# Sliding-window attention and feed-forward on one core: scores of six blocks in two steps, the mask table later, the order laid anew

## The chip, the cores and the metric

The kernel runs on one core of a Trainium2 chip. The metric is device time in microseconds (us), the median of several executions. Five engines work side by side, each through its own list of instructions, in order: TensorE (PE) multiplies matrices into PSUM, ScalarE (ACT) evaluates functions, VectorE (DVE) and GpSimd (POOL) work elementwise, SyncE (SP) issues transfers. ACT and POOL can issue transfers too.

## What is computed

Attention of 8 heads over 8 sequences of 576 rows, each row seeing itself and the 127 rows before it, with a bias that falls linearly with distance; then a normalised two-layer feed-forward part with a residual.

```python
# q, k, v: (8, 8, 576, 64) float32; scale = 1 / sqrt(64); window = 128
scores = scale * np.matmul(q, k.transpose(0, 1, 3, 2))
rel = pos[:, None] - pos[None, :]
slopes = 2.0 ** (-8.0 * (np.arange(H) + 1) / H)
bias = slopes[:, None, None] * (-np.abs(rel))[None]
mask = (rel >= 0) & (rel < window)
scores = np.where(mask, scores + bias, -1e9)
attn = softmax(scores)                      # (written out in the reference)
x = np.matmul(attn, v)                      # heads side by side: (8, 576, 512)
xn = (x - mean) / np.sqrt(var + 1e-06) * g_ln
out = x + np.maximum(xn @ w_ch1, 0.0) @ w_ch2     # w_ch1: 512 x 2048, w_ch2: 2048 x 512
```

## The kernel before

The 4608 rows are 36 blocks of 128 rows. Attention goes block by block; the feed-forward part goes by chunks of two to four blocks (`CHUNKS`). Every piece of work is a task with its dependencies, a rank `v` and assumed costs; a small planner in the kernel places the tasks on the engines, and the instructions are emitted in the order that it finds. So constants such as costs, ranks and `PICK` (which engine may do a task of which block) alter the order of the whole program. While PE would have nothing to do in the first 26 us of the plan, the kernel puts in filler matmuls on `warm_t`.

For one block (cut):

```python
CHUNKS = [2, 3, 4, 3, 4, 4, 4, 4, 4, 4]
BY_BIAS = 6       # blocks 0 to 5: the bias and mask come by a matmul (Z)
QK_BY_DMA = 13    # from this block on q and k are transposed by DMA, not by PE
X_BY_DMA = 11     # the same for x
SPANS = [0, 2, 5, 7]   # pairs of blocks whose q and k come in one transfer

scs = [psum.tile([P, 2, 512], FP32, ...) for n in range(2)]   # two score tiles
fb = {n: psum.tile([P, 512], FP32, ...) for n in range(4)}    # four banks for all else
plan.banks["sc"] = [0]      # both score tiles are handed out as one

# q, k, v loaded (SP), cast to 16 bit (POOL or ACT), q and k transposed on PE
# into a bank of fb, copied into qkt (DVE or ACT); then:

def e_s(e, b):                       # scores of both halves (four heads each)
    for half in range(2):
        for slot in range(2):
            for side in (() if r == 0 else (0,)) + (1,):   # block before, own block
                for g in range(2):
                    nc.tensor.matmul(scs[half][:, g, c0 : c0 + P], kt[rows, 1, hp, :],
                                     qkt[i][rows, 0, hp, :], start=not bias, stop=True, ...)
def e_z(e, b):                       # bias: scaled identity times distance table
    for half in range(2):
        for slot in range(2):
            for g in range(2):
                nc.tensor.matmul(scs[half][:, g, ...], sid[:, h, :], dist_t[:, kind, lo:],
                                 start=slot == 0, stop=False, ...)
if bias:
    z_ = [add(f"Z{i}", ("PE", ...), e_z, ..., acq=("sc", f"S{i}"))]
s_ = add(f"S{i}", ("PE", ...), e_s, z_ + qkt_done[i] + prev, ..., acq=("sc", f"S{i}"))
for half in range(2):
    # exp of one half: score tile -> probs (ACT)
    ex = add(..., e_x, [s_], ..., rel=f"S{i}")     # both give the score tiles back
    # from block 6 on: probs *= mask table (DVE or POOL)
# value products of each half (pv, PE), division (DVE), statistics, xs = (x - mean) * g (DVE),
# xs transposed (PE, then ACT or DVE; or by DMA) into xt
```

The mask table is made by ACT (eight instructions, `mreg`) and copied and cleared in two variants by POOL:

```python
for bank in range(4):
    for slot in range(2):
        # emit: nc.scalar.activation(mreg[:, bank, slot, :], dist_t[:, 0, :], AF.Exp, scale=-slope)
        tm.append(add(f"mreg{bank}{slot}", ("ACT", 0.4), emit, [d_dist[0]], av(MASK_AT, -10.0)))
# mmix and mnew: four copies and three memsets on POOL, which depend on tm
```

The weights come in eight transfers that POOL issues, which also convert to 16 bit; each stands behind a named cast:

```python
W_AFTER = [8, 14, 14, 14, 17, 18, 18, 20]   # 3 * block + (0: q, 1: k, 2: v)
# n < 4: a quarter of w1; n >= 4: a quarter of w2
```

The feed-forward part of a chunk (cut):

```python
for f in range(16):
    # A: 4 matmuls w1sb[:, kb, f] x xt[c] into a bank of fb; then relu -> ht (ACT or DVE)
for j in range(nb):
    # B: 16 matmuls ht x w2sb into a bank, in groups of four; then
    # ot = bank * rstd + xb (DVE), and the store (SP)
```

Of the kernel before, what the change touches and what calls it, by code (L numbers as in the profile page):

```python
# [16 lines left out]
class Task:  # L17
    __slots__ = ("eng", "emit", "deps", "v", "lat", "acq", "rel", "left", "users", "ready", "end", "start", "name", "room")

    def __init__(self, name, eng, emit, deps, v, lat, acq, rel):  # L20
        self.name, self.eng, self.emit, self.v, self.lat = name, eng, emit, v, lat
        self.deps = [d for d in deps if d is not None]
        self.acq, self.rel = acq, rel
        self.users, self.ready, self.end, self.start, self.room = [], 0.0, None, None, 0.0
# [22 lines left out]
class Plan:  # L47
# [36 lines left out]

    SLACK = (0, 0.4, 0)

# [13 lines left out]
    def run(self):  # L100
# [36 lines left out]
        def bank(t):  # L137
            if t.acq is None or t.acq[1] in held:
                return True, None
            open_ = [(when, b) for b, when in state[t.acq[0]].items() if when is not None and when <= now + 1e-9]  # L140
            return (True, min(open_)[1]) if open_ else (False, None)

        while left:
# [10 lines left out]
            for e in engines:  # L154
# [24 lines left out]
                if t.room:  # L179
                    used["DMA " + e] += t.room  # L180
                if t.acq is not None and t.acq[1] not in held:
                    held[t.acq[1]] = (t.acq[0], b)
                    state[t.acq[0]][b] = None
                if t.rel is not None:
                    waits[t.rel] -= 1
                    if waits[t.rel] == 0:
# [3 lines left out]
                        n += 1  # L190
                self.order.append((t, e, held[t.acq[1]][1] if t.acq is not None else None))
                left -= 1
# [26 lines left out]
def kernel(  # L219
# [10 lines left out]
    nc = tc.nc  # L230
# [12 lines left out]
    CH = CB * P  # L243
    CHUNKS = [2, 3, 4, 3, 4, 4, 4, 4, 4, 4]
    FIRST = [sum(CHUNKS[:c]) for c in range(len(CHUNKS))]
# [24 lines left out]
    SPAN = 36.0  # L270
    LEAD = 1.45
    WARM = 26.0
    SPANS = [0, 2, 5, 7]
    SLACK = (0.1, 0.4, 0.5)
    PICK = {('xt', 0): 'ACT DVE', ('xt', 8): 'ACT', ('cv', 5): 'POOL ACT', ('cv', 0): 'POOL', ('ev', 8): 'DVE', ('ev', 1): 'DVE', ('mkb', 8): 'DVE', ('mkb', 3): 'POOL', ('mka', 2): 'DVE', ('mkb', 4): 'POOL', ('ev', 3): 'ACT', ('mka', 0): 'DVE', ('ck', 8): 'ACT', ('mkb', 0): 'POOL', ('cq', 5): 'POOL', ('ev', 5): 'DVE', ('ck', 2): 'POOL', ('ck', 7): 'ACT', ('mkb', 6): 'POOL', ('mka', 5): 'DVE', ('cq', 6): 'POOL ACT', ('cq', 2): 'POOL ACT', ('xt', 6): 'ACT DVE', ('mka', 7): 'DVE', ('cq', 8): 'ACT', ('xt', 5): 'DVE', ('mka', 6): 'POOL', ('cv', 7): 'POOL ACT', ('cv', 3): 'POOL', ('xt', 3): 'ACT DVE', ('mka', 4): 'POOL', ('mka', 3): 'POOL', ('ev00', 4): 'DVE', ('cs1', 1): 'POOL', ('cs0', 0): 'POOL ACT', ('ev10', 3): 'DVE', ('xt', 2): 'ACT', ('cq', 3): 'POOL', ('cs0', 8): 'POOL ACT', ('ev01', 8): 'DVE', ('ev10', 8): 'ACT', ('ev11', 5): 'ACT', ('cs0', 2): 'POOL ACT', ('cq', 4): 'POOL', ('ev00', 8): 'DVE', ('ev01', 0): 'ACT', ('cv', 8): 'ACT', ('ev11', 0): 'ACT', ('cv', 4): 'POOL', ('mkb', 5): 'POOL', ('ev01', 6): 'DVE', ('cv', 6): 'ACT', ('ev10', 5): 'DVE ACT', ('cs1', 4): 'POOL ACT'}
    BY_BIAS = 6
    MASK_AT = 6
    QK_BY_DMA = 13
    X_BY_DMA = 11

# [45 lines left out]
    fb = {n: psum.tile([P, 512], FP32, tag=f"fb{n}", name=f"fb{n}") for n in range(4)}  # L326
    plan.banks["sc"] = [0]
    plan.banks["fb"] = list(fb)
# [18 lines left out]
    def load(name, src, r, i, v, slot=None):  # L347
        slot = i if slot is None else slot
        got = []
        for p0, n, b, s0 in where(i):  # L350
            def emit(e, bank, p0=p0, n=n, b=b, s0=s0):
                nc.sync.dma_start(  # L352
                    out=r[slot][p0 : p0 + n, :, :],
                    in_=src[b, :, s0 : s0 + n, :].rearrange("h p d -> p h d"),
                )
            t, d = plan.transfer(f"{name}{i}", "SP", 0.6, 1.22 * n / P, n / P, emit, (), v)
            r.writes(slot, t)
            got.append(d)
        return got
# [6 lines left out]
    for t in vx.tiles:  # L366
# [4 lines left out]
        plan.transfer(  # L371
            f"dist{n}", "ACT", 0.5, 0.15 * (k1 - k0), 0.0,
            lambda e, b, k0=k0, k1=k1: nc.scalar.dma_start(out=dist_t[:, k0:k1, :], in_=dist_dram.ap()[:, k0:k1, :]), deps, v,
# [25 lines left out]
    for bank in range(4):  # L399
        for slot in range(2):  # L400
            def emit(e, b, bank=bank, slot=slot):
                nc.scalar.activation(
                    out=mreg[:, bank, slot, :], in_=dist_t[:, 0, :], func=AF.Exp,
                    scale=-float(slopes[head_of(bank, slot)]),
                )
            tm.append(add(f"mreg{bank}{slot}", ("ACT", 0.4), emit, [d_dist[0]], av(MASK_AT, -10.0)))
    tmix, tnew = [], []
# [46 lines left out]

    W_AFTER = [8, 14, 14, 14, 17, 18, 18, 20]
    t_w = {}
# [14 lines left out]

    span_done = {}
    qkt_done, vx_done, aggr_done, xs_done, xt_done = {}, {}, {}, {}, {}

    def attention(i):
# [33 lines left out]
        if i in span_of:  # L509
            n = span_of[i]  # L510
            if SPANS[n] == i:
                evs = [[], []]
                for a, r_, w_ in ((0, qs, qs16), (1, ks, ks16)):
                    key = f"T{i}.{a}"

                    def e_c(e, b, r_=r_, w_=w_):
                        dst = w_[n][:, :, :, :]
                        src = r_[n][:, :, :].rearrange("p h (t d) -> p t h d", t=2)
                        if e == "POOL":
                            nc.gpsimd.tensor_copy(out=dst, in_=src)  # L520
                        else:
                            nc.scalar.activation(out=dst, in_=src, func=AF.Copy)
                    cs = add(f"c{key}", pick(f"cs{a}", "POOL", POOL=1.25, ACT=1.02), e_c, [span_load[n][a]], av(i, 0.1 * a))
                    r_.reads(n, cs); w_.writes(n, cs)

# [54 lines left out]

        def e_s(e, b):
            for half in range(2):
                for slot in range(2):
                    hp = 2 * half + slot
                    for side in (() if r == 0 else (0,)) + (1,):
                        for g in range(2):
                            rows = slice(D * g, D * g + D)
                            kt = qkt[i - 1 + side]
                            c0 = slot * 2 * P + side * P
                            nc.tensor.matmul(  # L590
                                scs[half][:, g, c0 : c0 + P],
                                kt[rows, 1, hp, :],
                                qkt[i][rows, 0, hp, :],
                                start=not bias,
                                stop=True,
                                skip_group_check=True,
                            )

        pr = []
        def e_z(e, b):  # L600
            for half in range(2):
                for slot in range(2):
                    for g in range(2):
                        h = head_of(2 * half + g, slot)
                        nc.tensor.matmul(
                            scs[half][:, g, slot * 2 * P + lo : slot * 2 * P + 2 * P],
                            sid[:, h, :],
                            dist_t[:, kind, lo:],
                            start=slot == 0,
                            stop=False,  # L610
                            skip_group_check=True,
                        )
        if bias:
            z_ = [add(f"Z{i}", ("PE", 0.87 if r else 0.46), e_z, t_sid + [d_dist[kind > 0]], av(i, 1.5), acq=("sc", f"S{i}"))]
        else:
            z_ = []
        s_ = add(f"S{i}", ("PE", 0.64 if r else 0.42), e_s, z_ + qkt_done[i] + prev, av(i, 2.0), acq=("sc", f"S{i}"))
        qkt.reads(i, s_)
        if r:
            qkt.reads(i - 1, s_)  # L620
        for half in range(2):

            def e_x(e, b, half=half):
# [5 lines left out]
                nc.scalar.activation(out=o, in_=n_, func=AF.Exp, scale=inv_sqrt_d)  # L629
            ex = add(f"ex{'ab'[half]}{i}", ("ACT", 1.02 if r else 0.62), e_x, [s_], av(i, 2.4 + half), rel=f"S{i}")  # L630
            probs.writes(i, ex)
# [12 lines left out]
        for half in range(2):  # L644
            key = f"V{'ab'[half]}{i}"

            def e_pv(e, b, half=half):
                pp = fb[b]
                for hh in range(4):
                    h = 4 * half + hh  # L650
                    bank, slot = 2 * half + h % 2, (h % 4) // 2
                    for side in (() if r == 0 else (0,)) + (1,):
# [8 lines left out]
                     [pr[half], cv] + ([vx_done[i - 1]] if r else []), av(i, 5.0 + half), acq=("fb", key))  # L661
            probs.reads(i, pv)
            vx.reads(i, pv)
            if r:
# [69 lines left out]
        if j == CHUNKS[c] - 1:  # L734
# [10 lines left out]
            lv.writes(c, ln); lv.reads(c, rs); mv.reads(c, ln); rstd.writes(c, rs)  # L745
            for n in range(nb):
                mv.reads(c, xs_done[FIRST[c] + n])
            kept[c] = rs
# [59 lines left out]
    for i in range(NBLK):  # L808
        attention(i)
    for c in range(len(CHUNKS)):  # L810
        mlp(c)
# [46 lines left out]
```

The softmax here doesn't subtract the row's maximum and nothing guards it: scores larger than these inputs give would overflow.

## Time and profile before

| | |
|---|---|
| time, median of 3 | 327.29 us (326.95 to 329.19) |
| span of the profiled execution | 326.8 us |
| PE busy | 317.4 us |
| ACT, DVE, POOL busy | 162.2, 186.0, 81.1 us |
| A (line 762), 640 matmuls | 135.2 us |
| B (line 788), 576 matmuls | 133.2 us |
| mean granted PE clock | 0.993 |
| HBM read, written | 36.93 MB, 9.44 MB |

The page gives busy times of the engines over the whole span and in 40 equal slices. The durations of matmuls overlap, so rates are read from runs of them in the timeline. A bracket behind a timeline row is the idle time before it and what ended it. Times of transfers run from issue to landing. Bias matmuls are line 605, scores 590, value products 653; transposes of q and k 530 (spans) and 555, of x 713; the filler is 817.

### The profile page before, as it was taken

The page shows a single profiled execution, that of the slowest core. Times are in us where ns is not written, and L with a number is a line of the kernel's source. Part 1 is how long each engine was busy: PE and PEld are TensorE (multiplying, and loading weights), DVE is VectorE, ACT ScalarE, POOL GpSimd, SP SyncE. Part 2 cuts the span into 40 slices and gives each one's busy share as a digit, 9 for nine tenths or more (in the row PEclk, how much of TensorE's full clock was granted, in tenths as well). Part 3 has the DMA queues.
Part 4 walks back from the last instruction along what each step waited for, and adds up shares of the span by engine and source line. Part 5 has one row for each costly group of instructions (what it writes and reads, how often), then busy time and mean ns, then how long its engine had stood idle before and what let it go on. Part 6 is the DMA issues. An engine that isn't in the chain of part 4 may idle for free.

```text
span 326.8 us, 6755 instructions
## 1 busy us (share of the span) xinstructions
PE 317.4 (97%) x2678; PEld 174.4 (53%) x2678; DVE 186.0 (57%) x402; ACT 162.2 (50%) x259; POOL 81.1 (25%) x116
## 2 busy tenths in 40 slices
PE   8996999999999999999999999999999999999995
PEld 7985865555554565454454544444444444444442
DVE  2284871797664299485685686566556745520011
ACT  5864964633760385376237632772276237405600
POOL 1775192443120431231600505210000000000000
PEclk9997999999999999999999999999999999999999
DMA  8999999997999999999999999934222320121011
GB/s 206 232 191 256 215 216 215 225 197 210 226 204 237 189 221 197 238 234 187 185 252 182 186 215 231 171 55 127 91 40 50 96 82 1 21 79 64 0 66 64
DMA packets 151955, 51.93 MB, mean 159 GB/s; under 512 B 134770, under 2 KB 147314, under 8 KB 151923
## 3 DMA queue, kind: packets, MB, share of 16 engines
q1 hardware_dynamic: 147264, 47.07, 69.1%
q0 software_dynamic: 4224, 4.19, 7.9%
q8 instruction: 21, 0.34, 0.5%
q10 hardware_dynamic: 434, 0.23, 0.3%
q14 instruction: 12, 0.09, 0.1%
HBM read 36.93 MB, written 9.44 MB: 142 GB/s over the span
## 4 chain that ended last, share of the span: by engine, by line
PE 84%; DMA 5%; SPq 4%; issue 2%; POOL 2%; DVE 0%; ACT 0%; POOLq 0%
PE fb L788 38%; PE fb L762 36%; PE sc L590 5%; PE fb L653 4%; DMA v<-in_v_dram 4%; SPq L352 3%; DMA k<-in_k_dram 1%; POOL probs L636 1%; SPq L428 1%; PE fb L555 1%; POOL w2sb L468 0%; PE fb L713 0%; PE fb L530 0%; ACT qkt L544 0%; DVE ot L796 0%
## 5 line engine op out<-in xcount | busy, mean ns | idle before, releaser
L762 PE MATMUL fb<-xt,w1sb 128*128 128x512 f16 (+2 forms) x640 | 135.2, 359 | 0.1
L788 PE MATMUL fb<-w2sb,ht 128*128 128x512 f16 x576 | 133.2, 379 | 0.0
L774 ACT ACTIVATE ht<-fb 128x512 f16<-128x512 f32 (+2 forms) x138 | 77.3, 562 | 92.6 <-PE fb L762 90.9
L762 PEld LDWEIGHTS <-w1sb 128*128 128x128 f16 x640 | 59.4, 98 | 56.1 <-issue 0.7
L629 ACT ACTIVATE probs<-sc 128x1024 f16<-128x1024 f32 (+1 forms) x72 | 67.8, 973 | 35.2 <-PE sc L590 32.6
L788 PEld LDWEIGHTS <-ht 128*128 128x128 f16 x576 | 53.4, 98 | 59.4
L796 DVE SCALAR_TENSOR_TENSOR ot<-fb,rstd,xb 128x512 f32<-128x512 f32 x36 | 26.9, 748 | 54.8 <-PE fb L788 54.4
L504 POOL CAST vx<-v 128x512 f16<-128x512 f32 x33 | 20.9, 638 | 112.9 <-PE fb L653 83.3
L636 DVE TENSOR_TENSOR probs<-probs,mreg 128x1024 f16<-128x1024 f16 (+1 forms) x46 | 31.3, 684 | 19.7 <-ACT probs L629 19.7
L673 DVE TENSOR_TENSOR xb<-fb,rec 128x256 f16<-128x256 f32 x72 | 30.0, 422 | 2.0
L653 PEld LDWEIGHTS <-probs 128*128 128x128 f16 x544 | 24.5, 98 | 11.8 <-POOL probs L636 0.7
L701 DVE SCALAR_TENSOR_TENSOR xs<-xb,mv,g_t 128x512 f16<-128x512 f16 x36 | 29.8, 829 | 1.1
L669 DVE RECIPROCAL rec<-fb 128x4 f32<-128x4 f32 x72 | 12.3, 176 | 28.7 <-PE fb L653 28.5
L653 PE MATMUL fb<-vx,probs 128*128 128x65 f16 x544 | 27.0, 194 | 0.4 <-POOL probs L636 0.4
L490 POOL CAST qk<-q 128x512 f16<-128x512 f32 x28 | 19.8, 709 | 29.1 <-DMA qkt<-qk 12.4
L690 DVE BATCH_NORM_STATS2 st<-xb 128x6 f32<-128x512 f16 x36 | 24.9, 691 | 0.9
L490 POOL CAST qk<-k 128x512 f16<-128x512 f32 x28 | 19.5, 695 | 9.0 <-DMA k<-in_k_dram 9.0
L590 PEld LDWEIGHTS <-qkt 64*128 64x128 f16 x544 | 15.6, 95 | 10.7 <-issue 9.6
L590 PE MATMUL sc<-qkt 64*128 64x128 f16 x288 | 19.7, 219 | 0.1
L590 PE MATMUL sc<-qkt,qkt 64*128 64x128 f16 x256 | 18.4, 221 | 0.0
L772 DVE TENSOR_SCALAR ht<-fb 128x512 f16<-128x512 f32 (+2 forms) x22 | 12.7, 579 | 6.5 <-PE fb L762 5.3
L817 PE MATMUL fb<-warm_t 128*128 128x128 f16 x176 | 13.3, 239 | 1.0 <-DVE warm_t L363 1.0
(47 smaller groups left out, 120.2 us busy)
## 6 DMA issues: line engine op xcount, KB each, us to landing
out_dram<-ot SPq DMA_DIRECT2D x36, 256.0 KB, 2.5
v<-in_v_dram SPq DMA_DIRECT2D x32, 256.0 KB, 4.9
q<-in_q_dram SPq DMA_DIRECT2D x24, 256.0 KB, 4.8
k<-in_k_dram SPq DMA_DIRECT2D x24, 256.0 KB, 4.6
qs<-in_q_dram SPq DMA_DIRECT2D x4, 512.0 KB, 7.6
ks<-in_k_dram SPq DMA_DIRECT2D x4, 512.0 KB, 8.2
w1sb<-in_moe_w_ch_dram POOLq DMA_DIRECT2D x4, 512.0 KB, 9.0
w2sb<-in_moe_w_ch_dram POOLq DMA_DIRECT2D x4, 512.0 KB, 9.7
```

The source lines that it names most:

```text
L490: en.tensor_copy(out=qk16[nrm[i]][:, a, :], in_=s)
L590: nc.tensor.matmul(scs[half][:, g, c0 : c0 + P], kt[rows, 1, hp, :], qkt[i][rows, 0, hp, :], start=not bias, stop=True, skip_group_check=True,
L629: nc.scalar.activation(out=o, in_=n_, func=AF.Exp, scale=inv_sqrt_d)
L636: en.tensor_tensor(out=pv, in0=pv, in1=mask[:, 2 * half : 2 * half + 2, :, lo:], op=ALU.mult)
L653: nc.tensor.matmul(pp[:, hh * (D + 1) : hh * (D + 1) + D + 1], probs[i][:, bank, slot, side * P : side * P + P], vx[i - 1 + side][:, h, 0 ...
L673: nc.vector.tensor_tensor(out=xb[i][:, 256 * half : 256 * half + 256].rearrange("p (h d) -> p h d", d=D), in0=pp[:, :, 0:D], in1=rec[2 * i ...
L690: nc.vector.bn_stats(out=st[i][:, :], in_=xb[i][:, :])
L701: nc.vector.scalar_tensor_tensor(out=xs[i][:, :], in0=xb[i][:, :], scalar=mv[c][:, j, 0:1], in1=g_t[:, :], op0=ALU.subtract, op1=ALU.mult,)
L762: nc.tensor.matmul(fb[b][:, 0:n_], w1sb[:, kb, f * P : f * P + P], xt[c][:, kb, 0:n_], start=(kb == 0), stop=(kb == NKB - 1),)
L774: nc.scalar.activation(out=ht[c][:, f, 0:n_], in_=src, func=AF.Relu)
L788: nc.tensor.matmul(pm[:, :], ht[c][:, f, j * P : j * P + P], w2sb[:, f, :], start=(f == 0), stop=(f == NFB - 1),)
L796: nc.vector.scalar_tensor_tensor(out=ot[i][:, :], in0=fb[plan.held[key][1]][:, :], scalar=rstd[c][:, j : j + 1], in1=xb[i][:, :], op0=ALU. ...
```

## The change

Four things are altered together.

- Each of the two score tiles is handed out by itself, and for blocks 0 to 5 the bias and scores of the two halves are separate tasks: the first half's exponential may start when its own scores are there, and the next block's bias may enter the first tile when that tile is read.
- The mask table's ACT instructions depend on block 1's value products, so that they no longer stand at the start of the program.
- The order is laid anew: other assumed costs of transfers and casts, other choices of engine, other places of the weights' transfers, chunks of other sizes at the start, rank offset `LEAD` 1.5 for 1.45.
- q and k are transposed by DMA from block 12 on instead of 13, x from block 13 on instead of 11.

The diff, cut (helpers of the planner that let a task take two tiles, and most of `PICK`, left out):

```diff
-    CHUNKS = [2, 3, 4, 3, 4, 4, 4, 4, 4, 4]
+    CHUNKS = [2, 3, 3, 4, 4, 4, 4, 4, 4, 4]
-    LEAD = 1.45
+    LEAD = 1.5
+    TABLE_AFTER = 1
+    SPLIT = 6
-    PICK = {... ('ck', 7): 'ACT', ('mkb', 6): 'POOL', ('ev00', 8): 'DVE' ...}
+    PICK = {... ('ck', 7): 'POOL ACT', ('mkb', 6): 'DVE', ('ev00', 8): 'DVE ACT', ...
+            ('ev', 0): 'ACT', ('cv', 2): 'POOL ACT', ('ev00', 2): 'ACT', ('ev00', 7): 'ACT', ('ev10', 2): 'DVE'}
-    QK_BY_DMA = 13
-    X_BY_DMA = 11
+    QK_BY_DMA = 12
+    X_BY_DMA = 13
-    plan.banks["sc"] = [0]
+    plan.banks["sc0"] = [0]
+    plan.banks["sc1"] = [0]
-            t, d = plan.transfer(f"{name}{i}", "SP", 0.6, 1.22 * n / P, n / P, emit, (), v)
+            t, d = plan.transfer(f"{name}{i}", "SP", 0.6, 1.24 if n == P else 0.76, n / P, emit, (), v)
-            tm.append(add(f"mreg{bank}{slot}", ("ACT", 0.4), emit, [d_dist[0]], av(MASK_AT, -10.0)))
+            tm.append(add(f"mreg{bank}{slot}", ("ACT", 0.4), emit, [d_dist[0]], av(MASK_AT, 0.0)))
-    W_AFTER = [8, 14, 14, 14, 17, 18, 18, 20]
+    W_AFTER = [11, 13, 14, 14, 17, 18, 18, 22]
...
-        if bias:
-            z_ = [add(f"Z{i}", ..., acq=("sc", f"S{i}"))]
-        s_ = add(f"S{i}", ..., z_ + qkt_done[i] + prev, av(i, 2.0), acq=("sc", f"S{i}"))
+        pr, s_ = [], {}
+        for halves in ((0,), (1,)) if i < SPLIT else ((0, 1),):
+            acq = [(f"sc{hf}", f"S{i}{hf}") for hf in halves]
+            if bias:
+                z_ = [add(f"Z{tag}{i}", ..., e_z(halves), ..., av(i, 1.5 + 0.6 * halves[0]), acq=acq)]
+            st_ = add(f"S{tag}{i}", ..., e_s(halves), z_ + qkt_done[i] + prev, av(i, 2.0 + 0.6 * halves[0]), acq=acq)
+            for half in halves:
+                s_[half] = st_
-            ex = add(..., e_x, [s_], av(i, 2.4 + half), rel=f"S{i}")
+            ex = add(..., e_x, [s_[half]], av(i, 2.4 + half), rel=f"S{i}{half}")
...
     for i in range(NBLK):
         attention(i)
+        if i == TABLE_AFTER:
+            for t in tm:
+                t.deps.append(pv_done[i])
```

## The prediction

> **What bounds the kernel now.** I read the page's first two parts, then the engines' busy time by stretches of 2.5 us, then the timelines of TensorE, ScalarE and GpSimd over the first 50 us, then landing times of single transfers (the DMA view cut to narrow windows).
>
> ```profile
> PE 317.4 (97%) x2678; PEld 174.4 (53%) x2678; DVE 186.0 (57%) x402; ACT 162.2 (50%) x259; POOL 81.1 (25%) x116
> ...
> PE   8996999999999999999999999999999999999995
> ```
>
> TensorE (PE) is at 9 in nearly every slice. Only the fourth slice (24.5 to 32.7 us) drops to 6, and the last to 5. So nothing in the middle can be won by removing waits; either work leaves PE, or the stretch ahead of the full load gets shorter. By stretches (us, then PE, PEld, DVE, ACT, POOL busy, granted clock, DMA share, GB/s):
>
> ```profile
> 22.50:25.00 2.50, 2.50 (x49) 2.13 (x46) 2.08 (x7) 1.41 (x2) 1.21 (x2) 1.00 1.14 285
> 25.00:27.50 2.50, 0.00 (x0) 0.00 (x0) 0.63 (x1) 0.53 (x1) 0.86 (x1) 1.00 1.23 278
> 27.50:30.00 2.50, 2.27 (x28) 1.93 (x29) 1.22 (x3) 0.84 (x2) 2.50 (x4) 0.77 1.25 207
> 30.00:32.50 2.50, 2.50 (x31) 1.98 (x30) 1.30 (x3) 1.45 (x3) 0.57 (x2) 0.55 1.22 267
> ```
>
> PE is idle for a whole stretch, and in the two after it gets 0.77 and 0.55 of its clock. Before 25 us it is only nominally full: much is filler on `warm_t`. PE's timeline (start, length, engine, line, operation, count, wait before):
>
> ```profile
> 23.71 1.29 PE L817 MATMUL fb<-warm_t 128*128 128x128 f16 x20
> 27.73 0.62 PE L530 MATMUL fb<-iden,qs 128*128 128x128 f16 x8 [2.73 <-POOL qs L520]
> ...
> 31.71 0.61 PE L762 MATMUL fb<-xt,w1sb 128*128 128x256 f16 x2
> ```
>
> The first product of the feed-forward part (A, line 762) starts at 31.71. The transposes at 27.73 belong to blocks 5 and 6, which A of the first chunk does not need, but PE takes its instructions in order, and everything behind them waits. GpSimd's timeline shows what they waited for:
>
> ```profile
> 18.09 0.88 POOL L466 DMA_DIRECT2D w1sb<-in_moe_w_ch_dram  x1
> ...
> 22.96 0.75 POOL L466 DMA_DIRECT2D w1sb<-in_moe_w_ch_dram  x1
> 26.64 1.04 POOL L520 CAST qs<-qs 128x1024 f16<-128x1024 f32 x1 [2.93 <-DMA qs<-in_q_dram]
> 27.62 1.48 POOL L466 DMA_DIRECT2D w1sb<-in_moe_w_ch_dram  x2
> ```
>
> The q span of blocks 5 and 6 had not landed. And ScalarE at the start:
>
> ```profile
> 5.23 1.95 ACT L402 ACTIVATE mreg<-dist_t 128x256 f16<-128x256 f16 x6 [3.21 <-DMA dist_t<-dist]
> 7.09 1.04 ACT L522 ACTIVATE qs<-qs 128x1024 f16<-128x1024 f32 x1
> ```
>
> The first q span was issued at 0.75 and took 4.2 us to land (4.95), but its cast waited behind six mask table instructions until 7.09.
>
> **What the Trainium skill says.** "DMA: Bandwidth & Descriptors", section "Issuing engines are not separate DMA queues": transfers started by different engines share the same 16 DMA engines and interleave. The trace agrees: the first q span landed in 4.2 us, the fourth, issued at 26.53 amid four weight transfers from GpSimd's queue, in 16.8. "TensorE: Matmul & The Clock Gate", section "What's actually happening": the array's clock halves after an idle window of about 3.4 us. Here 2.73 us without a matmul were enough for grants of 0.77 and 0.55. Same page, section "Back-to-back issue gap": a warm matmul of N columns costs N / 2.4 + 2.5 ns, 215.8 ns for 512. The trace's last 64 take 13.83 us, 0.216 each; I use such rates, not the 379 ns of the page's groups, which overlap.
>
> **The change, part by part.**
>
> *1. PE's work from the first A to the end.* I counted matmuls in the two built programs' orders and priced them from the timeline: A 0.108, 0.162, 0.216 us for 256, 384, 512 columns; B 0.216; score 0.0347 (16 in 0.55); value product 0.0325 (8 in 0.26); bias 0.109 (8 in 0.87); transposes 0.0565 (8 in 0.45) and 0.055 (4 in 0.22). Before: 286.9 us behind the first A. After: 286.6. Block 12's q and k transposes leave PE (8 x 0.0565 = 0.45 saved), those of x of blocks 11 and 12 come to it (8 x 0.055 = 0.44); four bias and eight value matmuls move ahead of A and eight span transposes behind it. Worth 0.3. Before really took 322.7 - 31.7 = 291.0, so gaps cost 4.1, which I keep except below.
>
> *2. When A starts.* The new order does not put the transposes of blocks 5 and 6 ahead of A; they stand behind its first 16 matmuls. So the 2.73 us wait no longer blocks. Filler falls from 176 to 138 matmuls, at 0.056 us 2.1 us that the author no longer expects to wait. By hand along ScalarE, with durations from its timeline (exponential 0.97, evacuation 0.67, table entry 0.33):
> - Block 0 doesn't move (score at 11.45): the cast of q goes to GpSimd, free at 4.95, but 48 + 21 filler matmuls stand ahead of its transposes, where 47 + 15 stood.
> - Block 1: its bias into the first tile needs only the first exponential; score at about 13.7 for 14.46, exponentials from 14.1 for 15.18.
> - Block 2: behind two evacuations, x's evacuation and two table entries, exponentials from 18.7 for 19.61. Here the table, now behind block 1's value products, gives back 0.66.
> - Block 3: from 21.5 for 23.59, with three table entries (1.0) between its halves, and two more behind the second.
> - Block 4: first half from 25.1, for 31.40, its value product at 26.3, four bias matmuls, then A at about **26.7** for 31.71. The first weights were issued at 18.09 behind the same cast in both orders and took 7.2 us: 25.3, just in time.
>
> Gain 5.0. With the idle gone the clock should not sag; before, A's first 16 matmuls took 2.17 for 1.73: another 0.4.
>
> *3. What then ends the wait: the arrivals.* Adding up PE work in each order from its first A gives how far in each arrival is needed. The value products and scores of later blocks and all eight weight slices must keep 5 us ahead of where they were. Landings before: w1 slices 25.3, 32.2, 36.4, about 39; w2 slices 44.5, 49.3, 54.5, 57.9 (issue start plus time to landing); q span of blocks 7 and 8 at 43.3. Needs after, with A at 26.7: w1 at 29.8, 33.7, 39.0; w2 at 46.6, 50.1, 53.6, 59.3; the q span's transposes at 41.8. The w1 slices should come 3 to 4 us earlier, since their issue no longer stands behind table clearing (second about 20.9 for 22.96) and the third and fourth not behind the late cast (about 22 to 24 for 27.62 to 28.3). But that starves the q and k spans and v on the SP queue, and DMA is at a share of 1.2 already: the bytes that have to land before block 7's transposes are the same. The span at 43.3 plus a cast of 1.04 is 44.3 against 41.8: 2.5 us late. The third w2 slice, behind a 2.1 us mask product on GpSimd, may land near 56 against 53.6: 2.4 late, but the same lateness, once paid. DMA ran at 158 to 170 GB/s from 15 to 22.5 us, and the earlier w1 issue fills some of that. I take a net loss of **2.0**.
>
> *4. Two score tiles and evacuations in the rest.* From block 6 on scores are issued as before. Nothing there ends PE's waits: no change. Chunks of 2, 3, 3, 4, ... for 2, 3, 4, 3, ... hold the same columns: none. The tail is the same 64 B matmuls and store: none.
>
> Sum: 5.0 + 0.3 + 0.4 - 2.0 = 3.7. 327.3 - 3.7 = **323.6 us**.
>
> **Rivals.** *Arrivals take it all:* DMA runs saturated from 22 us to about 200, and if the spans land no earlier and weights queue behind them, PE merely waits at 35 to 55 us instead of at 25: 326 to 327. For it: the 16.8 us landing and the share of 1.2. Against: PE had only 0.4 us of idle at 40 to 50, and 17 us of A work on chunks 0 and 1 fills time. *Everything is won:* the lateness in 3 is not there because DMA recovers its dip: 321.6. *ScalarE becomes the path:* eight table entries (2.6 us) now stand between exponentials of blocks 2 to 4; if evacuations slip too, A starts at 28.5 to 29: 325 to 326, unless it hides the arrivals' lateness. *Slower:* the new order, laid for other landings, holds PE behind an early instruction in the middle, as the span's transposes did: above 327. PE's 9s in every middle slice speak against a large one.
>
> **Range and chances.** Full gain gives 321.6 and a lost one 327. I set the range a little outside the first, since the 4.1 us of gaps may shrink too, and a little inside the second: 321.0 to 326.6. Over 2% faster needs less than 320.9: 0.07. Over 2% slower needs 334: 0.02. Within 2%: 0.91.
>
> **What would show it.** In the changed profile the first A should start at 26 to 28 us, no idle of PE above 1 us before it from 20 us on, the clock at 1.00 from 20 to 35 us; the fourth slice's 6 becomes 9. Step 3 is right if PE shows 1 to 3 us of idle between 30 and 60 us, ended by the span of blocks 7 and 8 or by w2. From first A to last B 289 to 293 us. The prediction is wrong if A starts after 29 us, if PE idles over 4 us later, or if the last B is not earlier by about A's advance less those waits.

## The result, and the profile after

The changed kernel takes 324.07 us (median of 4; 323.99 to 325.68) against 327.87 for the kernel before beside it: a ratio of 0.989, 95% interval 0.984 to 0.994. The profiled span is 322.2 us for 326.8. The medians fall by 3.8 us and the profiled spans by 4.6, because the profiled execution of the kernel before took 328.59 us, above its median, and that of the changed one 323.99.

TensorE by slices, from the page of the kernel after: the 6 in the fourth slice is gone.

```profile
PE   7989999999999999999999999999999999999994
```

The same stretches as before (us, then PE, PEld, DVE, ACT, POOL busy, clock, DMA share, GB/s):

```profile
22.50:25.00 2.50, 2.50 (x51) 2.02 (x48) 2.47 (x7) 2.50 (x8) 1.97 (x3) 1.00 1.19 234
25.00:27.50 2.50, 2.43 (x36) 2.01 (x34) 2.43 (x8) 2.50 (x5) 2.44 (x3) 1.00 1.21 222
27.50:30.00 2.50, 2.20 (x30) 1.80 (x29) 2.40 (x5) 1.46 (x5) 2.50 (x4) 1.00 1.21 207
30.00:32.50 2.50, 2.06 (x25) 1.67 (x22) 1.91 (x4) 1.97 (x6) 2.03 (x3) 1.00 1.21 197
```

The empty stretch is filled and the clock stays at 1.00. ScalarE and VectorE are now nearly full from 22.5 to 27.5 us. TensorE's timeline of the kernel after:

```profile
26.66 1.04 PE L781 MATMUL fb<-xt,w1sb 128*128 128x256 f16 x8
...
28.68 0.40 PE L732 MATMUL fb<-iden,xs 128*128 128x128 f16 x4 [0.30 <-DVE xs L720]
28.91 1.04 PE L781 MATMUL fb<-xt,w1sb 128*128 128x256 f16 x8
29.78 0.61 PE L538 MATMUL fb<-iden,qs 128*128 128x128 f16 x8
30.83 0.61 PE L781 MATMUL fb<-xt,w1sb 128*128 128x256 f16 x4 [0.44 <-DMA w1sb<-in_moe_w_ch_dram]
...
57.97 1.46 PE L781 MATMUL fb<-xt,w1sb 128*128 128x384 f16 x8 [0.34 <-DVE xt L740]
...
303.96 13.98 PE L807 MATMUL fb<-w2sb,ht 128*128 128x512 f16 x64
```

The first A starts at 26.66 for 31.71, 5.05 us earlier. The last B starts at 303.96; before, it was here:

```profile
308.72 13.98 PE L788 MATMUL fb<-w2sb,ht 128*128 128x512 f16 x64
```

That is 4.76 earlier. So nearly all of the advance reaches the end; 277.3 us lie between the two events now and 277.0 before. The brackets are all the waits of TensorE behind the first A that the profile lists: 0.30, 0.44 and 0.34 us.

### The profile page after: what moved, and what is told of

Read it like the earlier page. It is cut to its first block, busy times and chain, and to the rows that moved or that the text cites. A ratio compares the mean times of both kernels' runs of the same rounds, so it can differ in the third digit from the quotient of the medians.

```text
span 322.2 us, 6669 instructions
## 1 busy us (share of the span) xinstructions
PE 314.0 (97%) x2640; PEld 171.6 (53%) x2640; DVE 182.3 (57%) x398; ACT 162.6 (50%) x264; POOL 79.7 (25%) x116
## 4 chain that ended last, share of the span: by engine, by line
PE 85%; DMA 5%; SPq 4%; DVE 3%; issue 1%; ACT 0%; POOL 0%; DVEq 0%; POOLq 0%
PE fb L807 38%; PE fb L781 37%; PE sc L599 5%; PE fb L671 4%; DMA w1sb<-in_moe_w_ch_dram 3%; SPq L360 3%; DMA k<-in_k_dram 1%; SPq L436 1%; DVE probs L654 1%; DVE st L709 1%; PE fb L732 1%; DVE xs L720 0%; PE fb L563 0%; DVE xb L692 0%; DVE xt L740 0%
## 5 line engine op out<-in xcount | busy, mean ns | idle before, releaser
L793 ACT ACTIVATE ht<-fb 128x512 f16<-128x512 f32 (+2 forms) x142 | 78.9, 557 | 77.9 <-PE fb L781 76.6
L654 DVE TENSOR_TENSOR probs<-probs,mreg 128x1024 f16<-128x1024 f16 (+1 forms) x47 | 33.8, 729 | 20.7 <-ACT probs L647 20.4
L498 POOL CAST qk<-q 128x512 f16<-128x512 f32 x28 | 20.5, 731 | 49.6 <-DMA qkt<-qk 39.8
L720 DVE SCALAR_TENSOR_TENSOR xs<-xb,mv,g_t 128x512 f16<-128x512 f16 x36 | 28.5, 791 | 1.9 <-DMA xt<-xs 1.0
L498 POOL CAST qk<-k 128x512 f16<-128x512 f32 x28 | 18.6, 664 | 7.4 <-DMA k<-in_k_dram 6.7
L791 DVE TENSOR_SCALAR ht<-fb 128x512 f16<-128x512 f32 (+2 forms) x18 | 10.8, 606 | 15.4 <-PE fb L781 7.6
L839 PE MATMUL fb<-warm_t 128*128 128x128 f16 x138 | 10.8, 240 | 1.0 <-DVE warm_t L371 1.0
```

Source lines behind the costliest of these rows:

```text
L498: en.tensor_copy(out=qk16[nrm[i]][:, a, :], in_=s)
L654: en.tensor_tensor(out=pv, in0=pv, in1=mask[:, 2 * half : 2 * half + 2, :, lo:], op=ALU.mult)
L720: nc.vector.scalar_tensor_tensor(out=xs[i][:, :], in0=xb[i][:, :], scalar=mv[c][:, j, 0:1], in1=g_t[:, :], op0=ALU.subtract, op1=ALU.mult,)
L793: nc.scalar.activation(out=ht[c][:, f, 0:n_], in_=src, func=AF.Relu)
```

## The experiments

Two kinds were run. In the first, one part of the change is put into the kernel before or taken out of the changed one, and the kernel's planner lays its order again. In the second, the changed kernel's order is kept as it stands, and single instructions are moved in it. The results side by side; idle is TensorE's, from 25 to 80 us, 55 less its busy time. First A, idle and span are of one profiled execution. The ratio (with its 95% interval) compares the times of all executions but a few slow ones; where it and the span disagree, it is the better figure:

| run | order | first A, us | idle, us | span, us | ratio to before (interval) |
|---|---|---|---|---|---|
| before | | 31.71 | 3.3 | 326.8 | |
| after | | 26.66 | 1.2 | 322.2 | 0.989 (0.984 to 0.994) |
| t5late | new plan | 28.14 | 3.4 | 326.5 | 1.003 (1.001 to 1.005) |
| split_only | new plan | 29.84 | 2.3 | 325.0 | 0.995 (0.991 to 0.998) |
| table_only | new plan | 30.37 | 5.7 | 333.0 | 1.021 (1.017 to 1.026) |
| both_old_constants | new plan | 27.77 | 5.3 | 329.0 | 1.005 (1.002 to 1.007) |
| both_new_weights | new plan | 28.64 | 7.1 | 329.3 | 1.012 (1.006 to 1.017) |
| after_w0_early | new plan | 30.97 | 4.6 | 330.8 | 1.006 (1.002 to 1.010) |
| after_no_split | new plan | 29.65 | 3.5 | 335.5 | 1.023 (1.018 to 1.027) |
| after_table_first | new plan | 27.86 | 8.0 | 333.4 | 1.022 (1.018 to 1.026) |
| fixed_merged_scores | after's | 29.45 | 3.0 | 325.5 | 0.997 (0.994 to 0.999) |
| fixed_table_first | after's | 26.67 | 1.0 | 321.7 | 0.986 (0.983 to 0.988) |
| fixed_w0_early | after's | 26.50 | 1.9 | 322.7 | 0.989 (0.986 to 0.992) |
| fixed_lean | after's | 27.07 | 2.2 | 322.2 | 0.991 (0.987 to 0.994) |

### Is it only the span's transposes at the head of TensorE's list?

My theory from the prediction: TensorE stood behind a span that had not landed; move it away and most of the gain is there.

```diff
+                    if i == 5:
+                        late.append(tt)          # the span's transposes
...
+    for t in late:
+        t.deps.append(a_first[3])                # fourth group of A
```

> The kernel before, with one thing changed: the transposes of the span of blocks 5 and 6 depend on the fourth group of A, so they leave the place ahead of it. No split of the score tiles, no later table. Theory 1 (most of the gain is that PE no longer stands behind a q span that has not landed, plus the clock that sagged for it): first A at about 27.9 us for 31.71, clock 1.00 from 25 to 35 us, span about 323.8 (287.3 us priced behind the first A). Rival (the gain comes from the chain of exponentials and score tiles, so the wait just moves): first A at 30.5 or later, span 326 or more.

The first A came at 28.14 and the clock was 1.00 from 25 to 60 us, as theory 1 says, but the time did not fall: span 326.5, where theory 1 has 323.8. TensorE's timeline of this run shows where the advance went:

```profile
30.34 0.40 PE L715 MATMUL fb<-iden,xs 128*128 128x128 f16 x4 [0.71 <-DVE xs L703]
...
44.80 0.42 PE L655 MATMUL fb<-vx,probs 128*128 128x65 f16 x8 [0.41 <-POOL probs L638]
...
48.98 0.38 PE L715 MATMUL fb<-iden,xs 128*128 128x128 f16 x4 [0.94 <-DVE qkt L544]
...
56.80 0.81 PE L764 MATMUL fb<-xt,w1sb 128*128 128x384 f16 x4 [0.94 <-DVE qkt L544]
```

It is given back in pieces, 3.3 us in all, at transposes, value products and A groups behind which everything else on TensorE has to wait. So an early A is not enough; the pieces of attention laced between A's groups must be ready too.

### The parts of the change, with the order planned anew

```diff
     SPLIT = 6                       # split_only: this alone, on the kernel before
```

> The kernel before with the split of scores alone, table and all constants as before. In its order the span's transposes still stand ahead of the first A. Theory 1: PE still waits there until about 27.7, first A at about 29.2, span about 323.1 with 285.3 us priced behind A, a wait of 2 us or more ahead of the transposes, and a clock below 1.00 after it. Rival (chain of exponentials): the wait vanishes, first A before 28.0 us.

```diff
+        if i == 1:                      # table_only: this alone, on the kernel before
+            for t in tm:
+                t.deps.append(pv_done[i])
```

> The kernel before with the mask table behind block 1's value products alone. Span transposes still ahead of A, score tiles as one. Theory 1: PE waits at the span's transposes or at the fourth block's scores, first A at 29 to 30.5 us, span about 325. Rival (the table at the start of ScalarE was what held the start up): first A at 28 us or before.

```diff
     SPLIT = 6                       # both_old_constants: both, on the kernel before
     TABLE_AFTER = 1
```

> The kernel before with the split and the later table, all other constants as before (chunks, picks of engines, weights, transposes by DMA, assumed costs). Its order puts the span's transposes behind eight matmuls of A. Theory 1: first A at 26.7 to 27.2, span 322 to 322.5, as the changed kernel: the re-tuned constants bring nothing beyond. Rival (the constants matter, above all the weights' places): span 323.5 or more through idle of PE between 30 and 60 us.

The split alone gained 1.8 us of span. The wait at the span's transposes stayed, as theory 1 expected, but at 1.31 us for 2 or more and with the clock at 1.00 where theory 1 has less; A came at 29.84, 0.6 later than forecast. The later table alone lost 6.2 us, where a span of about 325 was expected, and both together lost 2.2 though A came at 27.77. My expectation for the last was wrong by 7 us. In that run TensorE waits 3.9 us for VectorE's normalisation. VectorE's timeline gives part of the reason (start, length, engine, line):

```profile
25.21 1.03 DVE L720 SCALAR_TENSOR_TENSOR xs<-xb,mv,g_t 128x512 f16<-128x512 f16 x1
...
28.30 1.44 DVE L720 SCALAR_TENSOR_TENSOR xs<-xb,mv,g_t 128x512 f16<-128x512 f16 x1
...
32.06 1.84 DVE L720 SCALAR_TENSOR_TENSOR xs<-xb,mv,g_t 128x512 f16<-128x512 f16 x1
```

GpSimd's timeline of the same run:

```profile
25.08 0.62 POOL L512 CAST vx<-v 128x512 f16<-128x512 f32 x1 [5.21 <-DMA v<-in_v_dram]
25.64 0.75 POOL L474 DMA_DIRECT2D w1sb<-in_moe_w_ch_dram  x1
...
28.09 1.05 POOL L530 CAST qs<-qs 128x1024 f16<-128x1024 f32 x1
29.07 1.56 POOL L420 COPY mmix<-mreg 128x1024 f16<-128x1024 f16 x1
...
32.30 2.49 POOL L420 COPY mnew<-mreg 128x1024 f16<-128x1024 f16 x2
```

The normalisation takes 0.75 us with GpSimd at rest (at 21.13 in this run) and up to 1.84 here, beside GpSimd's casts and table copies; the three together are 2.1 us longer. The rest of the 3.9 us is lateness that I did not trace, and the clock fell as well, to 0.50 from 35 to 37.5 us. And GpSimd waited 5.21 us for the v of block 4: the first weights, issued at 16.47 for 18.09, went ahead of it. That gave a second theory: the weights' places carry the rest of the change.

```diff
-    W_AFTER = [8, 14, 14, 14, 17, 18, 18, 20]     # both_new_weights, on the run before
+    W_AFTER = [11, 13, 14, 14, 17, 18, 18, 22]
```

> The kernel before with the split, the later table and the new places of the eight weight transfers; all other constants as before. Theory (the first weight transfer, issued 1.6 us too early once GpSimd is rid of the table, starved the load of block 4's v until 25 us and put the table's copies beside VectorE's normalisation): v of block 4 cast by 21.5 us, first A at 26.5 to 27.5, span 322 to 323. Rival (the engines' picks and assumed costs did it): span 325 or more.

```diff
-    W_AFTER = [11, 13, 14, 14, 17, 18, 18, 22]    # after_w0_early, on the changed kernel
+    W_AFTER = [8, 13, 14, 14, 17, 18, 18, 22]
```

> The changed kernel with the first weight transfer put back behind block 2's cast of v instead of block 3's; nothing else by hand. Theory of the weights' places: issue at about 16.4 for 17.9, v of block 4 cast at 24 us or later for 21.5, first A at 28 or later, span 325 or more for 322.2. Rival: within 0.7 us of the changed kernel.

```diff
-    SPLIT = 6                       # after_no_split, on the changed kernel
+    SPLIT = 0
```

> The changed kernel with the scores of every block as one task (no split). Filler rises from 138 to 188 matmuls. If the split is what frees the chain of exponentials: first A at 28.5 to 29.5, 287.9 us priced behind it, span 325 to 326. Rival (the weights' places carry all): first A by 27.5, span below 323.5.

```diff
-    TABLE_AFTER = 1                 # after_table_first, on the changed kernel
+    TABLE_AFTER = -1
```

> The changed kernel without the dependency of the mask table on block 1's value products: the table is made at the start, while ScalarE is free from 2 to 7 us. If moving the table is worth something: span 324 or more. My expectation: it is not, since the cast of the first q span left ScalarE: first A at about 27.3, 286.2 us priced behind it, span 322 to 323, and VectorE's normalisation at 0.75 us throughout, as GpSimd's copies come before 13 us.

The second theory failed its own test: in both_new_weights the v of block 4 was cast at 21.9 as wanted, and the run was still slower than before, with other waits (1.98 us at the span's transposes, which the new plan had put ahead of A again; 1.62 at block transposes at 63.66). after_w0_early did meet its figures (v of block 4 cast at 25.28, A at 30.97, span 330.8), and after_no_split had A near its forecast, at 29.65, but 9 us more span. after_table_first, where I expected 322 to 323, took 333.4. All four were slower than the kernel before, by 0.6 to 2.3%. after_table_first shows how: it begins almost as well as the changed kernel, and then, in TensorE's timeline,

```profile
31.91 0.61 PE L781 MATMUL fb<-xt,w1sb 128*128 128x256 f16 x4 [1.16 <-DMA w1sb<-in_moe_w_ch_dram]
44.23 0.81 PE L781 MATMUL fb<-xt,w1sb 128*128 128x384 f16 x4 [1.18 <-ACT ht L793]
47.72 1.03 PE L538 MATMUL fb<-iden,qs 128*128 128x128 f16 x8 [2.68 <-POOL qs L530]
```

an early instruction holds up all behind it, this time for the span of blocks 7 and 8, and the clock was 0.83 from 40 to 60 us. after_no_split and after_w0_early also lost 4.6 and 2.0 us of TensorE's time between 160 and 240 us, where no edit was made. A run of this kind therefore measures the edit plus a wholly new order, and the second can be larger: it doesn't tell what a part is worth. The parts had to be tried with the order held.

### The parts, with the changed kernel's order held

The list of tasks that the planner returns, filler included, is kept and single entries are moved before anything is emitted.

```diff
+    for i in range(6):                            # fixed_merged_scores
+        move(f"Za{i}", lambda: at(f"Zb{i}"))      # first half's bias to the second's
+        move(f"Sa{i}", lambda: at(f"Sb{i}"))      # scores likewise
+        if at(f"exa{i}") < at(f"Sa{i}"):
+            move(f"exa{i}", lambda: at(f"Sb{i}") + 1)
```

> The changed kernel's own order kept as it stands; only the split is undone within it: each first half's bias and scores stand directly ahead of the second half's, and where needed its exponential behind them. If the split itself frees the chain of exponentials: scores of blocks 3 and 4 each 1 to 1.5 us later, first A at 28 to 29.5 for 26.66, span 323.5 to 325 (part of the delay is hidden, since A then no longer waits for the second weight slice). Rival (the split is worth nothing once the order is good): first A by 27.2, span within 0.5 us of 322.2.

A came at 29.45, 2.8 us later, and the span rose by 3.3 to 325.5, a little beyond the range expected. TensorE now waits three times for exponentials before A (its timeline):

```profile
24.71 0.42 PE L671 MATMUL fb<-vx,probs 128*128 128x65 f16 x8 [0.90 <-ACT probs L647]
26.23 0.42 PE L671 MATMUL fb<-vx,probs 128*128 128x65 f16 x8 [0.83 <-ACT probs L647]
...
29.20 0.41 PE L671 MATMUL fb<-vx,probs 128*128 128x65 f16 x8 [0.90 <-ACT probs L647]
```

The first exponentials of blocks 3 and 4 start at 23.63 and 28.12 us, for 21.55 and 24.89 with the split. The three waits, 2.6 us, are what the split removes. In this order, it is worth 3.3 of the 4.6 us by the profiled spans. Other executions agree: at a mean clock of 0.999 or more the median spans are 325.9 us for the kernel before, 325.0 for this run and 322.3 for the changed kernel (only two executions), so 2.7 of 3.6. An order laid for whole scores might hide part of the waits; that was not tried.

```diff
+    for bank in range(4):                         # fixed_table_first
+        for slot in range(2):
+            move(f"mreg{bank}{slot}", lambda: at("Gc"))
+    for name in ("mmixc0", "mmixc1", "mnewc0", "mnewc1"):
+        move(name, lambda: at("cT2.1"))
```

> The changed kernel's own order kept; only the eight mask table instructions go back to ScalarE's start (free from 2 to 7 us) and GpSimd's four table copies to its gap from 10.6 to 14.5 us. If the later table is worth something: slower than 322.2 by 0.5 or more. My expectation: ScalarE sheds 2.6 us between exponentials, VectorE's normalisation beside the copies falls from 1.57 to 0.75 us, first A at 25.4 to 26 where the first weight slice (25.3) bounds it; but the second slice still lands at about 30.8, so the wait for it grows from 0.4 to 1.5 us and the span stays within 0.5 us of 322.2.

Span 321.7, within 0.5 as expected, so the later table is worth nothing here; but the way was another. A did not move (26.67): TensorE had no wait from 18.51 to 29.66 us, so its own list, filler included, and not ScalarE set it. No wait for the second slice came. The normalisation was 0.74 to 0.77 us throughout. The intervals of this run and of the changed kernel overlap, so I do not call it faster.

```diff
+    move("w0.i", lambda: at("cv3"))               # fixed_w0_early
```

> The changed kernel's own order kept; only the first weight transfer is issued one cast earlier, ahead of block 3's cast of v (about 16.4 for 17.9). Theory that it starves the load of block 4's v: that cast at 24 to 25.5 us for 21.45, the third weight slice and the cast of the q span some 3 us later, span 323.5 to 326. Rival (the weight's place does not matter, the re-planned orders lost for other reasons): v cast by 22.5 us, span within 0.5 us of 322.2.

Half right. GpSimd's timeline:

```profile
16.42 0.88 POOL L474 DMA_DIRECT2D w1sb<-in_moe_w_ch_dram  x1
...
24.91 0.61 POOL L512 CAST vx<-v 128x512 f16<-128x512 f32 x1 [4.40 <-DMA v<-in_v_dram]
...
29.06 1.03 POOL L530 CAST qs<-qs 128x1024 f16<-128x1024 f32 x1
```

The cast of v came 3.5 us later and the span's 3.0, but the order has slack there: TensorE waited 0.60 us at the span's transposes, and the span ended at 322.7, below the range.

```diff
+    lean = ("T0.0", "Za3", "Sa4")                 # fixed_lean, on fixed_table_first
+    # the filler directly ahead of these three tasks is dropped
```

> The changed kernel's own order with the table first, as in the run before, and 43 of the 138 filler matmuls left out: the 21 ahead of the first transposes, the 17 ahead of block 3's bias and the 5 ahead of block 4's scores. If TensorE's own place in its list (and not exponentials or arrivals) holds the scores back: block 0's scores 1.2 us earlier, first A at 25.4 to 26.2 for 26.67, span 320.7 to 321.4 for 321.7. Rival (the arrivals of the k span of blocks 2 and 3 and of the first weight slice bound it): first A at 26.4 or later, span 321.4 or more; and if the gaps let the clock sag, above 322.

The rival was right on A. TensorE was ready for it at 26.1 and then waited, in its timeline:

```profile
27.07 1.05 PE L781 MATMUL fb<-xt,w1sb 128*128 128x256 f16 x8 [0.96 <-DMA w1sb<-in_moe_w_ch_dram]
```

The first weights, issued at 17.91, took 9.1 us and landed at 27.0. In the changed kernel they were issued at 17.94, took 7.4 and landed at 25.3, 1.3 us ahead of A. So their landing bounds A here and not there; why they took longer here was not tried. The clock was 1.00 in this profiled execution, but 0.986 to 0.995 in the other five, with spans of 323.8 to 325.2 us. That is the expectation's "above 322" for a clock that sags. Most executions of the kernel before, taken beside it, were at 0.989 to 0.995 too, so it is not shown that the missing filler is the cause. Without this filler nothing was gained.

## Why the prediction was right

The time fell into the range (324.07, forecast 323.6), and the steps can be checked one by one.

*TensorE's work behind the first A.* 286.9 and 286.6 us priced, "worth 0.3". The stretch from the first A to the last B is 277.0 and 277.3 us, priced at 273.1 and 272.8. Gaps were 3.9 and 4.5. To the end of the last B it is 291.3 us, forecast 289 to 293. The rates held. One was cited too simply: the Trainium skill, "TensorE: Matmul & The Clock Gate", section "Back-to-back issue gap", gives N / 2.4 + 2.5 ns for an isolated matmul, and 131 ns for one of 512 columns in a sustained stream. The trace's 0.216 us in a stream of 64 fits the first and not the second.

*First A.* Forecast 26.7, measured 26.66, and the chain along ScalarE held too: scores of block 1 at 13.95 (13.7), exponentials of block 2 at 19.14 (18.7), of block 3 at 21.55 (21.5), of block 4 at 24.89 (25.1). No link is off by more than 0.5 us. Of this the clock's recovery is part: 1.00 in both stretches that had 0.77 and 0.55. My 0.4 for it counts only A's first 16 matmuls; it looks larger, and the kernel before does not lose it in every execution. Of 83 executions of the kernel before, taken beside the experiments, 26 had a mean clock of 0.999 or more, with a median span of 325.9 us, and 48 had 0.995 or less, with 327.4. The profiled one had 0.993.

*What I gave as the reason was incomplete.* The prediction said that with the span's transposes behind A "the 2.73 us wait no longer blocks", as if their place were the cause. fixed_merged_scores left them behind A and still lost 3.3 of 4.6 us, so their place alone does not do it: in this order the split carries most. t5late, which moved just those, got A at 28.14 and gained nothing, but it has a new plan. Whether their place is needed was not tried with the order held. The remaining 1.3 us lie in the rest of the order and in the clock, and which entry earns them was not tried.

*Arrivals.* The step "I take a net loss of 2.0" was the mis-sized term. The stretch from the first A to the last B grew by 0.3 us, although my other two terms take 0.7 off it; that leaves a loss of about 1.0, by estimate from these figures. I had also said 1 to 3 us of idle, ended by the span of blocks 7 and 8 or by w2. TensorE waited for neither. It waited 0.44 us for the second slice of w1, which landed at 30.8, 1.4 us earlier than before and not 3 to 4. I had the span's cast done at 44.3 us; it ran here:

```profile
39.83 1.04 POOL L530 CAST qs<-qs 128x1024 f16<-128x1024 f32 x1 [1.86 <-DMA qs<-in_q_dram]
```

The span was issued at 28.33 and landed in 11.4 us, for 26.53 and 16.8 before. In the kernel before, three weight transfers were issued while it was under way (two from 27.62 on, one at 32.63). In the changed one all of w1 had been issued by 23.91 and the first slice of w2 came at 37.23, and from 20 to 22.5 us the DMA engines moved 247 GB/s for 160. I had kept the landing of before although the order of issue changed. That this order is what brought the span in earlier is argued; no run changed it alone. All three waits behind A add up to 1.1 us where before had 0.4, nearer to the rival "Everything is won" than to my 2.0.

*Luck.* That 323.6 came so near to 324.07 is in part luck. With a loss of 1.0 the forecast would have been 322.6, and the kernel before took 327.87 us beside the changed one, not 327.3.

*Parts without effect.* The later table gave nothing back or forth in the held order, where I had charged 0.66 us to block 2. A run with only the transposes by DMA of q, k and x as before was not made.

*The rival of a slower new order* was put at "above 327" and dismissed by the 9s in the slices of before. The nine-tenths of the old order said nothing of a new one: seven of eight re-planned neighbours were slower than the kernel before.

## What to carry to other kernels

In a kernel whose order comes from a planner, test a part with the order held, by moving its entries in the finished list; a run with a new plan mixes the part with everything else that moved, and here the two differed by 8 us (medians of 335.4 against 327.2 without the split). An instruction that starts early on an in-order engine gains only if all that is laced between it and the end of the stretch is ready as well. When one transfer is moved, work out anew when those behind it land, in both directions.

## What the runs showed of the hardware

VectorE's normalisation has two inputs in SBUF (`xb` and `g_t`), and takes 0.75 us alone. In the changed kernel one of them started with a pair of GpSimd copies and took twice that, and the pair took 2.49 us where it takes 2.02 alone (timelines of VectorE and GpSimd):

```profile
27.05 1.57 DVE L720 SCALAR_TENSOR_TENSOR xs<-xb,mv,g_t 128x512 f16<-128x512 f16 x1
```

```profile
27.03 2.49 POOL L420 COPY mnew<-mreg 128x1024 f16<-128x1024 f16 x2
```

In fixed_table_first one ran beside GpSimd's memsets, which only write, and took 0.75 (the same two timelines):

```profile
29.61 0.75 DVE L720 SCALAR_TENSOR_TENSOR xs<-xb,mv,g_t 128x512 f16<-128x512 f16 x1
```

```profile
29.54 0.53 POOL L423 MEMSET mmix<- 128x512 f16 x1
```

The Trainium skill, "SBUF — State Buffer", section "Who interferes with whom", says just this: a VectorE instruction with two SBUF inputs contends with a GpSimd instruction that reads SBUF, not with one that only writes. The traces agree; the prediction had left it out.

The clock did not sag after every gap. In the kernel before, 2.73 us without a matmul were followed by 0.77 and 0.55. In both_old_constants, 2.01 us that ended at 33.96 were followed by 0.50 and 0.83; in after_w0_early, 2.43 us that ended at 29.62 were followed by 1.00 up to 200 us. The stretches of these two runs, in this order (us, then PE, PEld, DVE, ACT, POOL busy, clock, DMA share, GB/s):

```profile
35.00:37.50 2.50, 2.50 (x16) 1.79 (x14) 0.80 (x2) 2.06 (x4) 2.50 (x5) 0.50 1.19 216
37.50:40.00 2.50, 2.50 (x29) 1.51 (x27) 0.97 (x3) 1.48 (x2) 0.55 (x1) 0.83 1.18 257
```

```profile
25.00:40.00 15.00, 11.57 (x141) 8.97 (x140) 11.73 (x20) 9.99 (x23) 11.98 (x15) 1.00 1.16 235
```

So the length of a single gap does not tell whether the clock falls. What does is not shown here.
